# Linear attention followed by a SiLU layer pair: the order of all work in chunks 1 to 8 taken from a table

## Chip, cores and metric

One core of one Trainium2 chip. The metric is device microseconds (us) of one execution, from the first instruction to the last as the device counts it; lower is better. Profiles are of one execution each, and their span is about 2 us shorter than the time of the same execution. A run's state is "fast" or "slow" (lower granted TensorE clock for most of the execution); only fast runs are compared.

## The reference, cut to what matters

```python
# q, k, v: (8 batches, 8 heads, 576, 64);  w_in: (512, 2048);  w_out: (2048, 512)
q_s = softmax(q, axis=-1)                 # over the 64 features
k_s = softmax(k, axis=2)                  # over the 576 positions
kv  = einsum('bhsd,bhse->bhde', k_s, v)   # 64 x 64 per head
x   = einsum('bhsd,bhde->bhse', q_s, kv)  # to 4608 tokens x 512
h   = x @ w_in
out = (h * sigmoid(h)) @ w_out
```

## The kernel before

The 4608 tokens are cut into nine chunks: chunk 0 has 576 tokens, chunk 1 has 448, the rest 512. In chunk `t` TensorE does the first layer of chunk `t`, the second layer of chunk `t-1`, and, up to chunk 6, the attention of batch `t+1`. The attention of one batch runs through every engine: ScalarE takes exponentials of q and k, VectorE sums them, GpSimd normalises q and casts v, a DMA transposes q, TensorE makes kv (`kv`) and q·kv (`xt`), and ScalarE copies the latter to `XT`.

From chunk 2 on both layers use a seven-product scheme (Strassen's, in Winograd's form): VectorE forms sums of the inputs (`xsum`, `presum`), TensorE makes seven products, and the results are combined from PSUM by VectorE. First-layer blocks that don't use the scheme are called `mm1`. In these traces each engine takes its own instructions in program order, so the program order decides what an engine waits with. The program gives six PSUM banks to the ring from which `mm1`, `product1`, `kv` and `xt` draw, and two to the second layer.

```python
def product1(t, g, k):                  # one of seven first-layer products
    ...                                 # matmuls into a bank, then at once:
    if k == 1:                          # copy out of PSUM, ScalarE or VectorE
        if g in COPY_V: nc.vector.tensor_scalar_mul(out=new("s1"), in0=o, scalar1=1.0)
        else:           nc.scalar.activation(out=new("s1"), in_=o, func=ACT.Copy, scale=1.0)
    elif k == 6: add(new("u2"), MP[t, g, "s1"])      # VectorE: PSUM + SBUF
    elif k == 7: add(new("u3"), MP[t, g, "s1"])
    elif k == 2: silu(o, 0, 0)                       # ScalarE
    else:
        x = MP[t, g, {5: "u3", 4: "s1", 3: "u2"}[k]]
        add(x, x)                                    # VectorE, and its SiLU at once
        silu(x, *{5: (1, 1), 4: (1, 0), 3: (0, 1)}[k])
... # cut: the same pattern in product/after for layer two, stores through the SP queue

for b in range(4, B):   # what is done beside chunk b-1, by position in its list of units
    plan_attn(b, lambda i, f: plan(b - 1, i, f),
              (1, 1, 1, 1),   # four exponentials (q, q, k, k)
              (8, 10),        # q sums and q normalisations
              (6, 9),         # v casts
              11,             # DMA transpose of q
              (13, 16),       # kv products and their copies
              (20, 22),       # q.kv products and their copies
              11, 12)         # load of the next q; loads of the next k and v
```

The softmax here doesn't subtract the row's maximum and nothing guards it: scores larger than these inputs give would overflow.

## Time and profile before

| | before |
|---|---|
| time, median of 4 fast runs | 299.43 us (297.78 to 300.28) |
| span of the profile | 298.7 us |
| TensorE busy | 265.3 us, 89% |
| VectorE / ScalarE / GpSimd busy | 71% / 58% / 23% |

The first lines are of the page's first two parts: busy time by engine, and the granted TensorE clock in 40 equal slices (about 7.5 us each; 9 is 90% or more).

```profile
PE 265.3 (89%) x2546; PEld 187.6 (63%) x2546; DVE 211.0 (71%) x410; ACT 172.0 (58%) x275; POOL 69.7 (23%) x53
...
PEclk9999999997999689999999999999999999999999
```

TensorE idles 33 us, and the clock dips twice in mid-kernel, in slice 10 (67 to 75 us) and in slices 14 and 15 (97 to 112 us), each time at a pause of TensorE. The list of who TensorE waited for (total us, number of times, longest):

```profile
PE o L189 <- DMA qT<-eq: 9.3, 5, 5.5
PE hps L287 <- ACT s L315: 2.9, 4, 0.7
PE kvps L155 <- POOL vaug L100: 2.8, 1, 2.8
...
PE ops L379 <- ACT s L401: 2.1, 4, 0.5
...
PE hps L287 <- DVE s L313: 1.9, 4, 0.5
PE hps L287 <- DVE u L301: 1.4, 5, 0.6
```

`o` is q·kv, `qT` the transposed q, `hps` and `ops` the banks of layers one and two, `kvps` that of kv, `vaug` the cast v; `s` and `u` are PSUM copies and sums.

*Chunk 2.* The timeline of the DMA issues on the SP queue, around the longest wait (start, duration, what):

```profile
92.48 0.58 SPq L84 DMA_DIRECT2D qt<-in_q_dram  x1
93.17 5.93 SPq L124 DMA_TRANSPOSE qT<-eq  x1
```

and of TensorE, where q·kv starts at last:

```profile
102.56 0.48 PE L189 MATMUL o<-qT,kvn 64*64 64x320 bf16 x4 [5.51 <-DMA qT<-eq]
```

*Chunk 1.* GpSimd's timeline. `TW` are differences of weights; the gate holds GpSimd until VectorE has made its own weight differences `TX`.

```profile
54.17 0.17 POOL L614 CAST gate<-TX 1x1 f32<-1x1 bf16 x1 [16.10 <-DVE TX L262]
54.31 4.20 POOL L355 TENSOR_TENSOR TW<-W 128x1024 bf16<-128x1024 bf16 x2
58.48 4.21 POOL L355 TENSOR_TENSOR TW<-W,TW 128x1024 bf16<-128x1024 bf16 x2
62.65 4.18 POOL L113 TENSOR_TENSOR eq<-eq,rzq 128x1152 bf16<-128x1152 bf16 x2
66.79 2.24 POOL L100 CAST vaug<-vt 128x1152 bf16<-128x1152 f32 x2
```

kv needs the first cast; TensorE stands from 65.2 to 68.0.

*All chunks.* Length of each chunk, from its first first-layer matmul to the next chunk's (the last runs to the end of the span). It is read from the timeline of TensorE, and it is the measure used throughout:

| chunk | 0 | 1 | 2 | 3 | 4 | 5 | 6 | 7 | 8 and end |
|---|---|---|---|---|---|---|---|---|---|
| before, us | 32.6 | 27.1 | 30.6 | 31.4 | 30.2 | 31.2 | 30.2 | 25.8 | 43.3 |

Chunk 7 has the same products without kv and exponentials; chunks 3 to 6 are about 5 us longer, and some 1 us of that is kv.

### The profile page before, as it was taken

How to read it: one execution, taken by the hardware profiler on the slowest of the kernel's cores; microseconds unless marked ns; L12 is line 12 of the kernel's file. 1: busy time of each engine (PE TensorE's matmuls, PEld its weight loads, DVE VectorE, ACT ScalarE, POOL GpSimd, SP SyncE). 2: the span in 40 equal slices, each digit the busy share in tenths (PEclk: the TensorE clock that was granted, in tenths of full speed). 3: DMA queues.
4: the chain of work that ended last, by engine and by line, in shares of the span. 5: the costliest groups of instructions: out<-in, count | busy, mean ns of one | idle time of the engine just before them, and what ended most of it. 6: DMA issues, size and time to landing. Idle time of an engine off the chain costs nothing.

```text
span 298.7 us, 6269 instructions
## 1 busy us (share of the span) xinstructions
PE 265.3 (89%) x2546; PEld 187.6 (63%) x2546; DVE 211.0 (71%) x410; ACT 172.0 (58%) x275; POOL 69.7 (23%) x53
## 2 busy tenths in 40 slices
PE   8699989978989298879889988899899999999993
PEld 3366654434437156767677767676677787688782
DVE  3885767953256396968798879778788868867841
ACT  4774655842894388546955695459546456535300
POOL 0640400799362000700060016002420000000000
PEclk9999999997999689999999999999999999999999
DMA  7999999939409964089506970792052211301234
GB/s 241 297 200 279 307 256 322 343 126 234 163 0 220 221 254 160 1 151 379 170 2 121 333 232 13 119 341 81 0 102 63 59 38 35 72 1 37 70 72 105
DMA packets 42381, 46.48 MB, mean 156 GB/s; under 512 B 18544, under 2 KB 29808, under 8 KB 42352
## 3 DMA queue, kind: packets, MB, share of 16 engines
q1 hardware_dynamic: 37312, 38.35, 45.7%
q0 software_dynamic: 5040, 7.73, 11.7%
q8 instruction: 20, 0.33, 0.4%
q14 instruction: 9, 0.07, 0.1%
HBM read 36.70 MB, written 9.44 MB: 154 GB/s over the span
## 4 chain that ended last, share of the span: by engine, by line
PE 33%; DMA 19%; ACT 15%; DVE 13%; POOL 8%; issue 6%; SPq 3%; POOLq 1%; DVEq 0%; ACTq 0%
PE ops L379 15%; PE hps L287 8%; DMA W<-in_moe_w_out_dram 7%; DMA qT<-eq 7%; PE hps L209 5%; POOL eq L113 4%; PE ops L438 4%; DVE zq L107 4%; ACT ek L93 4%; ACT eq L93 3%; DVE u L301 3%; DMA kt<-in_k_dram 2%; ACT GT L234 2%; ACT L234 2%; DVE u L396 2%
## 5 line engine op out<-in xcount | busy, mean ns | idle before, releaser
L209 PE MATMUL hps<-XT,W 128*128 128x512 bf16 (+3 forms) x320 | 63.4, 338 | 1.8 <-ACT GT L234 1.3
L309 ACT ACTIVATE GT<-u 128x512 bf16<-128x512 f32 x40 | 25.1, 630 | 49.7 <-DVE u L301 49.7
L379 PEld LDWEIGHTS <-GT 128*128 128x128 bf16 x448 | 43.8, 98 | 10.4 <-issue 2.8
L209 PEld LDWEIGHTS <-W 128*128 128x128 bf16 x320 | 30.9, 98 | 26.4 <-issue 3.9
L113 POOL TENSOR_TENSOR eq<-eq,rzq 128x1152 bf16<-128x1152 bf16 x14 | 29.6, 2115 | 53.6 <-DVE rzq L108 35.2
L301 DVE SCALAR_TENSOR_TENSOR u<-hps,s 128x512 f32<-128x512 f32 x40 | 27.2, 683 | 18.5 <-PE hps L287 8.2
L379 PEld LDWEIGHTS <-SW 128*128 128x128 bf16 x336 | 32.8, 98 | 4.0 <-DVE SW L339 0.2
L287 PE MATMUL hps<-XS,TX 128*128 128x256 bf16 x240 | 34.6, 273 | 0.8 <-DVE u L301 0.8
L287 PEld LDWEIGHTS <-TX 128*128 128x128 bf16 x320 | 30.7, 99 | 7.0 <-issue 3.0
L230 DVE SCALAR_TENSOR_TENSOR GT<-sg,hps 128x320 bf16<-128x320 f32 (+3 forms) x64 | 23.7, 413 | 15.8 <-ACT sg L218 15.8
L438 PE MATMUL ops<-W,GT 128*128 128x512 bf16 x128 | 33.7, 387 | 1.1 <-DMA W<-in_moe_w_out_dram 0.9
L218 ACT ACTIVATE sg<-hps 128x320 f32<-128x320 f32 (+2 forms) x48 | 21.3, 454 | 20.2 <-PE hps L209 14.9
L379 PE MATMUL ops<-W,GT 128*128 128x256 bf16 x224 | 28.7, 272 | 2.1 <-ACT s L401 2.1
L287 PEld LDWEIGHTS <-W 128*128 128x128 bf16 x240 | 23.1, 99 | 11.6 <-issue 8.0
L100 POOL CAST vaug<-vt 128x1152 bf16<-128x1152 f32 x12 | 14.6, 1224 | 65.7 <-DMA vt<-in_v_dram 50.3
L379 PE MATMUL ops<-TW,SW 128*128 128x256 bf16 x224 | 28.8, 273 | 0.0
L301 DVE SCALAR_TENSOR_TENSOR u<-hps,u 128x512 f32<-128x512 f32 x40 | 27.0, 678 | 2.6 <-PE hps L287 1.8
L379 PE MATMUL ops<-TW,GT 128*128 128x256 bf16 x224 | 28.7, 273 | 0.0
L287 PE MATMUL hps<-XT,W 128*128 128x256 bf16 x160 | 23.9, 273 | 4.8 <-ACT s L315 2.9
L107 DVE TENSOR_REDUCE zq<-eq 128x18 f32<-128x1152 bf16 x16 | 21.5, 1344 | 8.4 <-ACT eq L93 8.4
L200 ACT CAST XT<-o 128x512 bf16<-128x512 f32 (+3 forms) x36 | 18.4, 560 | 11.0 <-PE o L189 11.0
L438 PEld LDWEIGHTS <-GT 128*128 128x128 bf16 x128 | 12.5, 99 | 14.1 <-issue 2.5
(68 smaller groups left out, 350.5 us busy)
## 6 DMA issues: line engine op xcount, KB each, us to landing
qt<-in_q_dram SPq DMA_DIRECT2D x6, 1152.0 KB, 5.9
kt<-in_k_dram SPq DMA_DIRECT2D x6, 1152.0 KB, 6.4
vt<-in_v_dram SPq DMA_DIRECT2D x6, 1152.0 KB, 8.7
W<-in_moe_w_in_dram POOLq DMA_DIRECT2D x4, 512.0 KB, 10.2
W<-in_moe_w_out_dram POOLq DMA_DIRECT2D x4, 512.0 KB, 17.8
out_dram<-oq SPq DMA_DIRECT2D x16, 128.0 KB, 3.6
out_dram<-u SPq DMA_DIRECT2D x30, 64.0 KB, 2.1
out_dram<-u SPq DMA_DIRECT2D x13, 128.0 KB, 2.4
```

What stands on the lines that cost most here:

```text
L93: nc.scalar.activation(out=o, in_=jgd(st[b][src], cc), func=ACT.Exp)
L107: nc.vector.reduce_sum(out=st[b]["zq"][:, cc], in_=e, axis=AX.X)
L113: eng.tensor_tensor(out=e, in0=e, in1=r[:, :, :, None].to_broadcast([128, J, 2, D]), op=ALU.mult)
L200: nc.scalar.copy(out=x, in_=o1[g][:, 0:size])
L209: nc.tensor.matmul(out=hps[:, 0:size], lhsT=W1[:, c, fb * 128:(fb + 1) * 128], rhs=XT[t][:, c, off:off + size], start=(c == 0), stop=(c == ...
L218: nc.scalar.activation(out=sg[:, 0:size], in_=hps[:, 0:size], func=ACT.Tanh, scale=0.5)
L230: nc.vector.scalar_tensor_tensor(out=y, in0=sg[:, h], scalar=1.0, in1=hps[:, h], op0=ALU.add, op1=ALU.mult)
L287: nc.tensor.matmul(out=o[:, f, :], lhsT=l(c, 2 * g + f), rhs=r(c), start=bool(first and f == 0 and c == 0), stop=(c == HK - 1), skip_group ...
L301: nc.vector.scalar_tensor_tensor(out=out, in0=o, scalar=1.0, in1=x, op0=ALU.mult, op1=ALU.add)
L309: nc.scalar.activation(out=y, in_=x, func=ACT.Silu)
L379: nc.tensor.matmul(out=o[:, a, :], lhsT=l(f), rhs=r(f), start=bool(first and a == 0 and f == 0), stop=(f == HF - 1), skip_group_check=True,)
L438: nc.tensor.matmul(out=OP[t, tb], lhsT=GT[t][:, fc, tb * 128:(tb + 1) * 128], rhs=W2[:, fc, :], start=(fc == 0), stop=(fc == NFB - 1),)
```

## The change

The intent: all of chunks 1 to 8 is placed by a table. Each chunk gives a position for every piece of work, and pieces that were glued together (a product, its sum, its SiLU, its store) get positions of their own. The core of the diff:

```diff
+STEADY = {'std': 1, 'order': [(1, 1), (1, 6), (1, 2), (1, 7), (1, 5), (2, 1), ...],
+  'ex': [-5.1, -2.59, -3.08, -3.57],          # exponentials q, q, k, k
+  'qs': [6.4, 6.9], 'qn': [6.91, 6.91], 'vs': [3.4, 9.92], 'tp': 7.9,
+  'lq': 10.95, 'lk': 13.9, 'lv': 11.41,       # loads of the next q, k, v
+  'sl': [0.5, 2.0, 6.5, 4.0],                 # SiLUs of the four plain blocks
+  'act': {(1, 5): 11.02, (1, 2): 6.55, ...},  # SiLUs held back
+  'xs': [-2.6, 0.4, 2.4, 1.9], 'pb': [-0.55, 0.46, 2.95, 1.46, 2.95], ...}
+for _t in range(3, 8):
+    PLAN[_t] = STEADY
+TXAT = [(0, 15.76), (0, 15.96), (1, -2.6), (1, -8.1)]          # VectorE's TX
+GATE = (1, 2.8)
+TWAT = [(1, 2.4), (1, 4.9), (1, 7.9), (1, 4.9), (1, 14.95), ...] # GpSimd's TW
... # tables of chunks 0, 1, 2, 8, 9 cut
-            if g in COPY_V:
+            if PLAN[t]["s1"][g]:        # one more copy per steady chunk on VectorE
... # product1 split into product1, sum1, silu1; mm1 into mm1, act1;
... # xt into xt, xtcopy; product into product, after
+    for l in todo:
+        for _, _, f, args in sorted(l, key=lambda x: x[:2]):
+            f(*args)
```

A position of -5.1 sorts to the front of the chunk's own list.

## The prediction

> **What bounds it now.** TensorE: busy 265.3 of 298.7 us (page, part 1). Its idle time (list of waits, timeline of its matmuls) falls into places that an order can reach:
>
> - Chunk 2: 5.5 us for the transposed q (DMA), whose issue at 93.17 took 5.93 us because a whole q load entered the same queue 0.7 us earlier. The granted clock falls to 0.68 in 100 to 110 us: an estimated 3 us more. The Trainium skill, "TensorE: Matmul & The Clock Gate", Part 1, says one idle window of about 3.4 us halves the clock; the trace agrees.
> - Chunk 1: 2.8 us for GpSimd's cast of v, behind four weight sums (2.1 us each) and two q normalisations that began only at 54.2 us, since a gate waits for a VectorE difference; a slow clock follows (0.88 in 70 to 80 us, about 1.5 us). At 87.8, 1.3 us for a SiLU: ScalarE was in 7 us of table loads and exponentials.
> - Chunks 3 to 6 last 31.4, 30.2, 31.2, 30.2 us (starts of their first matmuls); chunk 7, without attention, 25.8. Attention is about 1.3 us of matmuls, so about 27 is the floor. Each repeats the same waits: 0.5 + 0.2 + 0.5 + 0.3 + 0.7 behind the exponentials at its second position, and 0.4 to 1.6 for the transposed q; start to start, 3.4 to 4.5 us.
> - Chunks 7, 8: only 1 us. Start (17 us) and end (20 us) are not touched.
>
> **What the change does.** It adds no work, and places production, evacuation, SiLU and stores separately. Exponentials stand before the chunk (-5 to -2.6); q sum, normalisation and transpose move from positions 8 to 11 to 6.4 to 7.9, about 3 us earlier; from chunk 2 on the transpose precedes the q load; S sums move away from the v cast (a 0.41 us sum took 1.37 us beside it); SiLUs wait behind copies and sums that free banks. One more PSUM copy (0.68 us) per steady chunk goes to VectorE. GpSimd's weight sums are spread. Chunk 0 is nearly the old order rewritten.
>
> **What it costs.** VectorE is busy 24.9 us per steady chunk (busy time by stretch), ScalarE 20. At 27 us VectorE would be 92% busy, so I do not expect the floor; holding sums back also keeps some of the six banks. Estimate: 28 us.
>
> **Sum.** Chunks 3 to 6: 4 x 2.7 = 11. Chunk 2: 6 of about 9. Chunk 1: 3 of about 5.5. Chunks 7, 8: 0.5. Together about 20 us, nearly all on the critical path, since TensorE is the chain. Predicted 280 us, 8 in 10 between 273 and 289. Faster by over 2%: 0.92; within: 0.06; slower: 0.02.
>
> **What would show it.** TensorE's idle time about 15 instead of 33 us; no wait of q·kv on the transpose over 1 us; the transpose's issue in chunk 2 near 3 us; clock at least 0.95 everywhere after 20 us; steady chunks 28 us apart; VectorE near 90% in them; table loads still 12; time before 50 us unchanged.
>
> **What would make it wrong.** (a) VectorE or ScalarE, in strict order, is blocked by an early sum or exponential whose data is late (k load), and steady chunks stay near 30. (b) A bank held back stalls the ring. (c) In chunk 2 the k exponentials lie between SiLUs, so the 1.3 us wait returns. (d) In chunk 1 the q load still precedes the transpose. If all bite, 290; if the order fits perfectly, 270.

## More of the kernel before

Asked by stretch, the granted clock is 0.50 from 68.9 to 72.3 us and from 99.6 to 106.4 us.

*Chunk 4, one of the four steady ones (3 to 6).* ScalarE's timeline:

```profile
139.81 0.58 ACT L234 ACTIVATE GT<-hps 128x512 bf16<-128x512 f32 x1
140.40 1.28 ACT L93 ACT_TABLE_LOAD   x1
141.70 2.22 ACT L93 ACTIVATE eq<-qt 128x1152 bf16<-128x1152 f32 x2
143.82 2.20 ACT L93 ACTIVATE ek<-kt 128x1152 bf16<-128x1152 f32 x2
146.04 1.28 ACT L234 ACT_TABLE_LOAD   x1
147.33 1.57 ACT L234 ACTIVATE GT<-hps 128x512 bf16<-128x512 f32 x3
148.78 0.62 ACT L401 ACTIVATE s<-ops 128x512 f32<-128x512 f32 x1
```

The chunk's first matmul started at 138.18. The exponentials stand behind its first SiLU; the copy `s`, which frees a bank of layer two, comes 10.6 us after that matmul. Later in the same chunk comes one of the four waits of the list's second line, for a first-layer copy `s`:

```profile
152.33 0.63 ACT L309 ACTIVATE GT<-u 128x512 bf16<-128x512 f32 x1 [2.44 <-DVE u L301]
...
154.09 0.60 PE L287 MATMUL hps<-XT,W 128*128 128x256 bf16 x4 [0.73 <-ACT s L315]
```

The copy itself starts at 153.46, behind two SiLUs. These had waited 2.44 us for sums of VectorE, which stood behind a q sum (1.34 us, at 150.04) and, before it, behind a wait of VectorE for the layer-two copy (1.51 us). The 2.44 us and the 0.73 us are the same in all four steady chunks; chunks 7 and 8, without a q sum, don't have the wait.

## The result, and the profile after

| | before | after |
|---|---|---|
| time, median of 4 fast runs | 299.43 us | 276.84 us (276.09 to 278.42) |
| ratio | | 0.926 (95% interval 0.920 to 0.932) |
| span of the profile | 298.7 | 274.1 |
| TensorE busy / idle | 265.3 / 33.4 | 261.6 / 12.5 |

Ratios here are the mean time of one kernel's fast runs over that of the other's fast runs of the same rounds, so not quite the ratio of the medians quoted.

```profile
PE 261.6 (95%) x2546; PEld 186.8 (68%) x2546; DVE 218.1 (80%) x417; ACT 167.8 (61%) x268; POOL 70.4 (26%) x53
...
PEclk9979999999999999999999999999999999999998
```

TensorE's idle time falls by 20.9 us, and its busy time by 3.7 although it does the same work. The two dips of the clock in mid-kernel are gone; TensorE was busy for 7.2 us of them, at half the clock, an estimated loss of 3.6 us. The dip in the third slice, 3.4 us long, lies in chunk 0 and costs an estimated 1.7 us; a second profile of the same kernel, below, does not have it. The rest of the 3.7 us is not explained here. TensorE's longest waits now:

```profile
PE hps L317 <- ACT GT L264: 2.5, 3, 1.6
PE kvps L169 <- ACT vaug L112: 1.8, 2, 1.1
```

No wait over 0.2 us on the transposed q, on the cast v of chunk 1, or on a copy `s` is left; the first line is new. In chunk 2 the transpose goes before the q load, and its issue is half as long:

```profile
84.96 2.86 SPq L138 DMA_TRANSPOSE qT<-eq  x1
87.87 0.57 SPq L98 DMA_DIRECT2D qt<-in_q_dram  x1
```

In chunk 1 GpSimd starts three microseconds earlier, and two weight differences instead of four precede the normalisations:

```profile
50.98 0.84 POOL L644 CAST gate<-TX 1x1 f32<-1x1 bf16 x1 [9.64 <-DVE TX L292]
51.78 2.11 POOL L386 TENSOR_TENSOR TW<-W 128x1024 bf16<-128x1024 bf16 x1
53.97 2.13 POOL L386 TENSOR_TENSOR TW<-W,TW 128x1024 bf16<-128x1024 bf16 x1
57.49 4.20 POOL L127 TENSOR_TENSOR eq<-eq,rzq 128x1152 bf16<-128x1152 bf16 x2 [1.38 <-ACT sg L248]
61.64 2.13 POOL L386 TENSOR_TENSOR TW<-W,TW 128x1024 bf16<-128x1024 bf16 x1
63.71 2.25 POOL L114 CAST vaug<-vt 128x1152 bf16<-128x1152 f32 x2
```

ScalarE in chunk 4, whose first matmul starts at 122.29:

```profile
123.06 1.28 ACT L107 ACT_TABLE_LOAD   x1
124.35 1.16 ACT L107 ACTIVATE eq<-qt 128x1152 bf16<-128x1152 f32 x1
126.72 2.22 ACT L107 ACTIVATE ek<-kt 128x1152 bf16<-128x1152 f32 x2 [1.20 <-DMA kt<-in_k_dram]
128.84 1.15 ACT L107 ACTIVATE eq<-qt 128x1152 bf16<-128x1152 f32 x1
130.00 1.28 ACT L264 ACT_TABLE_LOAD   x1
131.30 1.09 ACT L264 ACTIVATE GT<-hps 128x512 bf16<-128x512 f32 x2
132.27 0.60 ACT L434 ACTIVATE s<-ops 128x512 f32<-128x512 f32 x1
```

Now `s` stands behind two SiLUs instead of four, and starts 10.0 us after the chunk's first matmul instead of 10.6. The exponentials start 2.1 us after it instead of 3.5. But ScalarE waits 1.2 us for the k load in mid-block (2.2 us in chunk 5), and the SiLUs behind it are what TensorE's new wait is for.

| chunk | 0 | 1 | 2 | 3 | 4 | 5 | 6 | 7 | 8 and end |
|---|---|---|---|---|---|---|---|---|---|
| before, us | 32.6 | 27.1 | 30.6 | 31.4 | 30.2 | 31.2 | 30.2 | 25.8 | 43.3 |
| after, us | 33.0 | 23.4 | 21.3 | 28.1 | 27.9 | 28.9 | 27.1 | 25.7 | 42.2 |
| gain | -0.4 | 3.7 | 9.3 | 3.4 | 2.3 | 2.3 | 3.0 | 0.0 | 1.0 |

So 11.0 of the 24.6 us of span lie in the four steady chunks, 9.3 in chunk 2 and 3.7 in chunk 1. The two profiled executions took 300.64 and 276.09 us, the one slower and the other faster than its kernel's median, so the profiles differ by 2 us more than the medians (22.6 us). The experiments ask which part of the table earned them.

### The profile page after: what moved, and what is told of

It reads as the page before. It is cut to its first block, busy times and chain, and to the rows that moved or that the text cites. A ratio compares the mean times of both kernels' runs of the same rounds, so it can differ in the third digit from the quotient of the medians.

```text
span 274.1 us, 6282 instructions
## 1 busy us (share of the span) xinstructions
PE 261.6 (95%) x2546; PEld 186.8 (68%) x2546; DVE 218.1 (80%) x417; ACT 167.8 (61%) x268; POOL 70.4 (26%) x53
## 4 chain that ended last, share of the span: by engine, by line
PE 61%; DMA 12%; ACT 8%; DVE 8%; SPq 4%; issue 3%; POOL 2%; ACTq 0%; POOLq 0%; DVEq 0%
PE ops L410 21%; PE hps L234 16%; PE hps L317 14%; DMA kt<-in_k_dram 9%; PE ops L474 8%; DMA vt<-in_v_dram 3%; ACT ek L107 2%; SPq L98 2%; PE kvps L169 2%; SPq L463 2%; DVE u L334 2%; ACT L264 1%; ACT eq L107 1%; POOL eq L127 1%; PE o L204 1%
## 5 line engine op out<-in xcount | busy, mean ns | idle before, releaser
L410 PEld LDWEIGHTS <-GT 128*128 128x128 bf16 x448 | 43.4, 98 | 8.6 <-issue 1.0
L234 PEld LDWEIGHTS <-W 128*128 128x128 bf16 x320 | 31.6, 100 | 25.5 <-issue 1.6
L334 DVE SCALAR_TENSOR_TENSOR u<-hps,s 128x512 f32<-128x512 f32 x40 | 27.1, 681 | 8.7 <-PE hps L317 6.4
L474 PE MATMUL ops<-W,GT 128*128 128x512 bf16 x128 | 31.8, 379 | 0.0
L248 ACT ACTIVATE sg<-hps 128x320 f32<-128x320 f32 (+2 forms) x48 | 21.3, 456 | 15.5 <-PE hps L234 10.4
L410 PE MATMUL ops<-TW,SW 128*128 128x256 bf16 x224 | 28.0, 273 | 0.0
L121 DVE TENSOR_REDUCE zq<-eq 128x18 f32<-128x1152 bf16 x16 | 21.3, 1329 | 4.9 <-ACT eq L107 4.9
L107 ACT ACTIVATE ek<-kt 128x1152 bf16<-128x1152 f32 x16 | 18.1, 1158 | 5.6 <-DMA kt<-in_k_dram 5.6
```

Of the source, the lines that this page charges most:

```text
L107: nc.scalar.activation(out=o, in_=jgd(st[b][src], cc), func=ACT.Exp)
L121: nc.vector.reduce_sum(out=st[b]["zq"][:, cc], in_=e, axis=AX.X)
L234: nc.tensor.matmul(out=hps[:, 0:size], lhsT=W1[:, c, fb * 128:(fb + 1) * 128], rhs=XT[t][:, c, off:off + size], start=(c == 0), stop=(c == ...
L248: nc.scalar.activation(out=sg[:, 0:size], in_=hps[:, 0:size], func=ACT.Tanh, scale=0.5)
L334: nc.vector.scalar_tensor_tensor(out=out, in0=o, scalar=1.0, in1=x, op0=ALU.mult, op1=ALU.add)
L410: nc.tensor.matmul(out=o[:, a, :], lhsT=l(f), rhs=r(f), start=bool(first and a == 0 and f == 0), stop=(f == HF - 1), skip_group_check=True,)
```

## The experiments

The theory held after the result, as in the prediction (A): the steady chunks gain because the exponentials no longer stand in second place, where their 7 us hold up copies and sums. Rivals: (B) the earlier transpose of q; (C) SiLUs held behind copies and sums. For chunks 2 and 1: the place of the q load, and GpSimd's order. They ran in three sets, each set on one chip and beside the kernel before: e3, e4, e5, e8 (301.0 us for the kernel before), e1, e2, e6, e7 (301.1) and e9 to e12 (300.4). The headings give these labels. Only the third set holds the new kernel itself (e9); in the first two, "slower" and "faster" are against its 276.84 us from another chip. By the ratios to the kernel before, which differ by 1.6 us between its own two sets of runs, e3 comes out 4.6 us faster than the new kernel, e4 2.4, e1 2.0 and e7 9.7 us slower. Single microseconds are therefore read from chunk lengths where that is possible. For the edits of the old order, the old order was first written as a table; its instructions then stand in the same order as those of the kernel before on every engine.

### e3: exponentials put back to second place

```diff
+STEADY['ex'] = [0.9, 0.901, 0.902, 0.903]
```

> The new order, with only the four exponentials of chunks 3 to 6 put back to second place in the chunk. Theory A (what the steady chunks gained, about 2.7 us each, comes mainly from having the exponentials in front): the waits of TensorE on s and u sums and copies come back, 1.5 to 2.2 us a chunk, 6 to 9 us in all, so 283 to 286 us. Theory B (it comes from the earlier transpose of q) and theory C (from holding SiLUs back): under 2 us slower, 277 to 279; and if the late k load is what limits the new order, it may even be equal, since the exponentials then no longer wait 1.2 to 2.2 us for k.

Measured: 274.09 us, ratio to before 0.911 (0.906 to 0.915), where the new kernel has 0.926. Chunks 3 to 6 took 28.1, 27.0, 27.8, 27.0 us. Putting the exponentials back makes the kernel 2.8 us *faster* than the new order's 276.84, on a chip where the kernel before was 1.5 us slower. Theory A falls: the place of the exponentials is not what was gained. ScalarE's wait for k fell from 5.6 to 2.0 us over the whole run, as the rival had allowed; the front place had only moved the exponentials ahead of their data. In time the two places are close: in chunk 4 the first exponential starts 3.0 us after the first matmul here and 2.1 us in the new kernel. What the front place is worth once k comes in time is not tested by itself; chunks 4 to 6 then take 26.8 us each (e12 below) against 27.0, 27.8 and 27.0 here, where ScalarE still waits some for k.

### e8: only the exponentials moved, in the old order

```diff
+for t in range(3, 7):
+    PLAN[t]['ex'] = [-5.1, -3.57, -3.08, -2.59]    # all else in the old order
```

> The old order (instruction for instruction that of the kernel before on every engine) with only the exponentials of chunks 3 to 6 moved in front of the chunk, in the order q, q, k, k. Theory A: the 2.2 us of waits behind the exponential block go, the waits on the transpose stay: 4 to 8 us faster than the kernel before, 291 to 295 us. Theories B and C: within 2 us of the kernel before.

Measured: 299.94 us, ratio 0.999 (0.992 to 1.006). No gain. TensorE's waits on `s` and `u` are about those of before (8.3 us in all, as before). ScalarE's timeline in its chunk 4 (first matmul at 140.67) says why:

```profile
141.76 0.63 ACT L407 ACTIVATE GT<-u 128x512 bf16<-128x512 f32 x1 [1.82 <-DVE u L385]
...
143.70 2.22 ACT L158 ACTIVATE eq<-qt 128x1152 bf16<-128x1152 f32 x2
...
149.34 2.06 ACT L315 ACTIVATE GT<-hps 128x512 bf16<-128x512 f32 x4
151.26 0.63 ACT L485 ACTIVATE s<-ops 128x512 f32<-128x512 f32 x1
```

ScalarE, in strict order, reaches the block only behind the last SiLU of the chunk before, which itself waits 1.8 us for VectorE. "In front of the chunk" thus moves the first exponential from 3.5 to 3.0 us after the chunk's first matmul, and one more SiLU then stands between the block and `s`: `s` still starts 10.6 us after that matmul. The run shows that this edit gains nothing; what exponentials that really start earlier would be worth it cannot show.

### e4: the transpose of q put back

```diff
+STEADY.update(qs=[7.9, 9.9], qn=[7.91, 9.91], tp=10.9)
```

> The new order, with only the q sums, q normalisations and the transpose of chunks 3 to 6 put back to their old places (7.9, 9.9, 10.9). Theory B (the earlier transpose is most of the gain): 6 us or more slower, 283 or more. Theory A: a wait of q.kv on the transpose of 0.5 to 1.5 us a chunk returns, so 1 to 4 us slower in all, 278 to 281, with no new waits on s and u sums.

Measured: 281.07 us, ratio 0.934 (0.929 to 0.938): 4.2 us slower than 276.84, just above what A allowed and below what B asked for. Chunks 3 to 6 sum to 117.2 us against 111.9 in the new kernel's profile. Two waits came:

```profile
PE o L205 <- DMA qT<-eq: 3.2, 3, 1.3
PE hps L318 <- DVE u L335: 2.2, 5, 0.5
```

The first was expected. The second was not: a q sum, 1.34 us on VectorE, now stands in front of a `u` sum for which TensorE waits. So the earlier q chain is worth 4 to 5 us of the steady chunks' 11 (2.4 by the ratios), in two ways.

### e5: SiLUs not held back

```diff
+STEADY.update(act={}, add={}, ya={}, sl=[0, 1, 2, 3])
```

> The new order, with every SiLU of chunks 3 to 6 issued straight behind what produces its input, and the last store sum as well. Theory C (holding SiLUs back is most of the gain): 5 us or more slower, 282 or more. Theory A: SiLUs wait in strict order for sums but ScalarE is only 65 to 70 percent busy, so within 1.5 us, 275.5 to 278.5.

Measured: 278.16 us (276.75 to 279.43), ratio 0.923 (0.917 to 0.929); by medians 1.3 us slower than 276.84, by ratio equal. It is not the main part (C falls as a whole), but its mechanism is plain; one wait of the kernel before returned, once in each steady chunk:

```profile
PE ops L411 <- ACT s L435: 3.1, 4, 0.9
```

Four SiLUs again stand in front of the copy that frees the layer-two bank. The profiled execution was the slowest of the four, and its steady chunks sum to 115.2 us, 3.3 more than the new kernel's; the medians say 1.3. About half of the difference is the clock: from 163.4 to 166.8 us it was 0.50 while TensorE was busy throughout, an estimated loss of 1.7 us, and the three other executions ran at a higher mean clock (0.995 to 1.0 against 0.985). So holding SiLUs is worth 1 to 2 us, up to 3 when the clock dips, and these runs don't fix it closer. (The edit's `add={}` changes nothing: in the steady table its entries name products that have no sum. The sums themselves were hardly held back.)

### e10: VectorE's input sums put back

```diff
+STEADY.update(xs=[-0.08, 0.92, 1.92, 2.92], pb=[0.915, 0.916, 1.915, 1.916, 2.915])
```

> The new order, with VectorE's S sums and layer-two sums at the start of chunks 3 to 6 put back to the old places (after the first, second and third first-layer block, in one row). Theory D (a part of the steady gain is that the s copy and u sums, which free PSUM banks, no longer stand behind eight bf16 sums on VectorE): a wait of TensorE of 0.6 to 0.9 us on VectorE's s copy and u sum returns in each chunk, 2 to 4 us slower than the new kernel. If the old places cost nothing in the new surroundings: under 0.7 us.

Measured: 276.33 us, beside 276.25 for the unchanged new kernel on the same chip (below). It costs nothing that can be told apart: TensorE's waits on VectorE's `u` and `s` rise from 0.2 to 0.8 us in all.

### e1: the q load in front of the transpose, in chunk 2 alone

```diff
+PLAN[2]['lq'] = 5.85        # was 5.95; the transpose stands at 5.9
```

> The new order, with one change in chunk 2: the load of the next q is issued just before the transpose of q, as in the kernel before, instead of just behind it. Theory A (the 5.9 us issue of the transpose before came from the q load in the same queue): the issue goes from 2.9 to 5 to 6 us, q.kv of chunk 3 waits 1.5 to 4 us for it, 1.5 to 4 us slower in all. Rival (the issue was long for another reason, such as stores or other loads): issue stays near 3 us and the time within 1 us.

Measured: 280.99 us, ratio 0.933 (0.930 to 0.936); 4.1 us slower than 276.84. The SP queue:

```profile
84.84 0.58 SPq L99 DMA_DIRECT2D qt<-in_q_dram  x1
85.54 5.77 SPq L139 DMA_TRANSPOSE qT<-eq  x1
```

The issue doubles from 2.86 to 5.77 us with nothing changed but the load in front of it, q·kv waits 2.7 us, and the clock falls to 0.7 and 0.8 in two slices. Chunk 2 grows from 21.3 to 25.7 us. That the load's place in front makes the issue long is shown. By what way is not: in chunk 0 the transpose's issue takes 4.7 to 6.0 us in both kernels and in this run with no load issued on that queue in the 33 us before, while other transfers keep the DMA engines busy, so traffic alone may do it.

### e2: the transpose in front of the q load, in the old order

```diff
+PLAN[2]['tp'] = PLAN[2]['lq'] - 0.0005     # all else in the old order
```

> The old order, with one change in chunk 2: the transpose of q is issued just before the load of the next q. Theory A: issue near 2.9 us at about 92.5, landing near 97.5 instead of 102.5, so q.kv waits 0.5 to 1.5 us instead of 5.5, the pause is too short to lower the clock: 5 to 8 us faster than before, 291 to 294.5. Rival (the exponentials and the normalisation of chunk 2 came too late, and the store issues in front of the transpose held it): 0 to 3 us faster, the low clock stays.

Measured: 297.18 us, ratio 0.988 (0.984 to 0.992): 3.9 us faster than the 301.12 beside it, between the two expectations. The issue took 2.84 us, q·kv waited 1.95 us, the clock stayed up. Chunk 2 shrank by 4.9 us, and chunk 3 grew by 0.9 (TensorE then waits there 1.5 us for `s`). So this one swap makes about half of chunk 2's 9.3 us. The rest goes with the earlier q exponentials and normalisation, as far as the traces tell: in the new kernel GpSimd ends them at 80.9, in the old at 90.2, and the wait for a SiLU of 1.3 us at 87.8 is gone. No run undid these.

### e7: the old weight differences in chunk 1, a first try

```diff
+TXAT[:] = [(0, 15.76), (0, 15.96), (1, 0.9), (1, 1.9)]
+TWAT[:] = [(1, 2.801)] * 4 + [(1, 11.801)] * 4
```

> The new order, with only the weight differences of chunks 0 and 1 (VectorE's four, the gate, GpSimd's eight) put back to their old places. Theory A (the v cast of chunk 1 came late behind four weight sums on GpSimd that began late): the wait of kv on the cast returns, 2 to 4 us, with a slow clock behind it: 3 to 5 us slower. Rival (chunk 1 gained by its exponentials and by the matmuls of the second layer put at its end): under 1 us.

Measured: 288.65 us, ratio 0.958 (0.955 to 0.962), 11.8 us slower, three times what was expected. The edit was not what it was meant to be: in the new table the v casts stand at 11.8 and 11.9, so four differences fell *between* them, which neither kernel has.

```profile
PE kvps L217 <- POOL vaug L162: 10.8, 2, 8.1
```

8.1 us of this is that artifact; the other wait, 2.7 us on the first cast, is the one of the kernel before.

### e11: the old weight differences, mended

```diff
+TXAT[:] = [(0, 15.74), (0, 15.96), (1, 0.9), (1, 1.9)]
+TWAT[:] = [(1, 2.801)] * 4 + [(1, 11.95)] * 4
```

> The first try at the old weight sums put four of GpSimd's sums between the two v casts of chunk 1, which neither kernel has, and cost 8.2 us there. This one is the old order of GpSimd: gate, four sums, two normalisations, both casts, four sums. The wait of kv on the cast should be 2.9 us as in the kernel before, chunk 1 should grow from 23.4 to 26 to 27.5 us, 3 to 4 us slower than the new kernel in all. If the first-layer blocks that come before kv cover the wait: under 1 us.

Measured: 281.18 us, median of the three fast runs from 280.19 to 282.26 (the fourth was slow); ratio 0.937 (0.931 to 0.943); 4.9 us slower than the unchanged new kernel beside it. GpSimd's order in chunk 1, with VectorE's differences that it waits for, is worth all of that chunk's 3.7 us and more. The profile (clock 0.85, span 303.7) cannot show how the 4.9 us divide. The profiles of the kernel before, of e2 and of e8, which all have the old weight differences, show the same two things: a wait of 2.8 us on the first cast and, within 1 us of its end, 3.4 us at a clock of 0.50, an estimated 1.7 us more.

### e9: the new kernel again

> The new kernel, unchanged, to stand on the same chip as the three beside it. 276 to 278 us; chunk lengths as in its first profile except where ScalarE waits for k, which may vary by 1 us a chunk with the loads.

Measured: 276.25 us, ratio 0.921 (0.916 to 0.925). Chunks 3 to 6: 28.1, 28.4, 27.7, 27.6 us, where the first profile had 28.1, 27.9, 28.9, 27.1: the sum is the same (111.7 and 111.9), the longest one moves with the wait for k.

### e6 and e12: the k load in front of the v load

Two runs, the first with the exponentials' order changed too.

```diff
+STEADY.update(lk=11.41, lv=13.9, ex=[-5.1, -3.57, -3.08, -2.59])   # first run
+PLAN[2].update(lk=6.4, lv=12.91)                                   # (as it was)
+STEADY.update(lk=11.41, lv=13.9)                                   # second run
```

> A try at a faster kernel: the new order, with the k load issued before the v load, in chunks 2 to 6, and the exponentials of chunks 3 to 6 in the order q, q, k, k. ScalarE waits 1.2 to 2.2 us for k in the new order and TensorE 0.5, 0.7 and 1.8 us behind that. If that wait is the cause, those go: 1.5 to 3 us faster than the new order, 274 to 275.5 us. If VectorE (90 percent busy) is what sets the chunk, within 0.7 us of it. It may also be that v, then late, holds the cast and kv back.

> The new order, with only the k load issued before the v load in chunks 3 to 5 (in chunk 2 it already is); the order of the exponentials, q, k, k, q, stays. If the order of the two loads is what made ScalarE wait for k: ScalarE's wait for k goes and steady chunks are 26.8 to 27.2 us, 3 to 4 us faster than the new kernel. If the order of the exponentials is needed too (k is asked for one exponential too early): 1 to 2 us faster, with waits for k of about 1 us left.

Measured: 272.51 us with both, ratio 0.905 (0.902 to 0.908); 272.74 us with the loads alone, ratio 0.909 (0.905 to 0.912), beside 276.25 for the new kernel on the same chip: 3.5 us faster. In both, chunks 4 to 6 take 26.8 us each. The order of the two loads is the whole of it; ScalarE in chunk 4 of the second run:

```profile
124.50 1.16 ACT L110 ACTIVATE eq<-qt 128x1152 bf16<-128x1152 f32 x1
125.57 2.20 ACT L110 ACTIVATE ek<-kt 128x1152 bf16<-128x1152 f32 x2
127.68 1.15 ACT L110 ACTIVATE eq<-qt 128x1152 bf16<-128x1152 f32 x1
```

No gap is left. These two are the fastest kernels. VectorE, at over 90% of a 26.8 us chunk, was not what held the new order at 28. In a stretch of one chunk's length TensorE is now busy throughout (columns as explained in the next section):

```profile
121.90:148.70 26.80, 26.80 (x303) 21.42 (x301) 24.39 (x47) 19.40 (x30) 7.08 (x4) 1.00 0.63 189
```

## Why the prediction was right, and where its reasons were not

280 us was predicted, 273 to 289 as the range; 276.84 was measured. Term by term, with what the chunk lengths show:

| term | predicted gain | measured |
|---|---|---|
| chunks 3 to 6 | 4 x 2.7 = 11 us | 11.0 |
| chunk 2 | 6 | 9.3 |
| chunk 1 | 3 | 3.7 |
| chunks 0, 7, 8 and end | 0.5 | 0.6 |

- **Bound by TensorE's waits: right.** Idle time was to be about 15 us and is 12.5. The signs named for it all came: no wait on the transpose, its issue 2.86 us in chunk 2, steady chunks 28.0 us apart in the mean, twelve table loads, the first 49 us unchanged, no dip of the clock after 20 us except in the last slice. VectorE's busy time in chunk 4, from the busy times by stretch, is 25.5 of 27.8 us, 92%:

```profile
122.30:150.10 27.80, 27.16 (x302) 21.39 (x300) 25.47 (x46) 19.45 (x30) 6.66 (x4) 1.00 0.65 184
```

  (The columns are stretch and length, then busy us of TensorE, its weight loads, VectorE, ScalarE and GpSimd, then clock, DMA share and GB/s.)
- **Steady chunks: the size right, a reason wrong.** The prediction put five of the waits "behind the exponentials at its second position". That step failed. Moved to the front in the old order, the exponentials gained nothing, and moved back in the new order they gained 2.8 us. In place of it the runs showed the earlier q chain (4.2 us, part of it because a q sum no longer stands in front of a `u` sum) and, with 1 to 3 us, the copy placed before two of the SiLUs. That 28 us a chunk came out as estimated is luck in part: the estimate gave VectorE's load as the limit, and what held the chunks there was the late k. Nothing that was undone brought back the wait of before on the first-layer copy `s` (2.9 us in all). Its chain in the kernel before, shown above, needs two things at once: SiLUs in front of the copy, and their sums behind a q sum. e5 put back the first alone (the SiLU there waits 1.3 us, TensorE not at all) and e4 the second alone (the copy then stands in front of the waiting SiLU). So the two changes together may have removed it, as may the new order of the products or the places of the second layer's products; no run puts both back, and that part of the 11 us stays open.
- **Chunk 2: the term mis-sized.** 6 us of "about 9" were claimed, and 9.3 came. The mechanism, a q load in front of the transpose, is shown in both directions (4.1 and 3.9 us of time, 4.4 and 4.9 us of chunk 2). The prediction held 3 us back, among other things for a SiLU wait that might return (its item c); none did. Its estimate of 3 us for the slow clock looks too large: the swap in the old order shortened the wait by 3.6 us and chunk 2 by 4.9, which leaves some 1.3 for the clock within that chunk. The trace of the kernel before agrees: of the 6.8 us at a clock of 0.50, TensorE was busy for only 3.8, an estimated loss of 1.9 us, since the dip had begun during the pause.
- **Chunk 1: right in kind.** 3 us were claimed, 3.7 came, and undoing the order of the weight differences alone costs 4.9.
- **The doubts.** The prediction named "exponentials in front of the chunk may wait for the k load", in its item (a). That happened, and cost 3.5 us by the last run. It held VectorE's load responsible for not reaching "about 27 is the floor"; that was wrong, for with the k load earlier the chunks reach 26.8 us.

Of the Trainium skill, "TensorE: Matmul & The Clock Gate", Part 1, says that an idle window of about 3.4 us halves the clock. It was used for the clock's dips. The runs agree on the half (0.50) and that a pause of 5.5 us brings it; but it also came with pauses of 2.7 and 2.8 us and, in e8, of 2.05 us, and not with one of 1.95 us, so the length of a single pause does not decide it here. "ScalarE: Activation LUTs", What ACT_TABLE_LOAD costs, gives 1283 ns for a table load; the traces show 1283 ns too.

## What to carry to other kernels

An instruction's place in the program is not its place in time: on an engine that runs in strict order, "earlier" starts no earlier than the wait in front of it ends, and data not yet there turns "earlier" into a stall for all that follows, so look first at what the instruction would wait for at its new place. On a queue shared by loads, stores and a transpose, put first what is needed first: two swaps of neighbouring DMA issues (transpose before q load, k load before v load) were worth about 4 and 3.5 us. When a table moves everything at once, a right total does not prove the reasons; undo the parts one by one, and compare the engine's order with both kernels before trusting such an undo.

## What the Trainium skill lacked or had wrong

- "DMA: Bandwidth & Descriptors", § DMA Transpose (X-bar), does not say what a plain load in front of a transpose does to it: with a 1152 KB load issued 0.7 us earlier on the same queue, the issue took 5.77 and 5.93 us, and 2.84 and 2.86 us with the load behind it. In chunk 0, with no load on that queue for 33 us but other transfers under way, it took 4.69 to 6.00 us.
- "TensorE: Matmul & The Clock Gate", Why this matters for your kernels, warns of idle gaps over about 3 us. Here a gap of 2.7 us (with one of 0.4 us that ended 0.7 us before it) went with a clock of 0.50 for 6.8 us, gaps of 2.8 us and one of 2.05 us with 3.4 us of it, and one of 1.95 us with none; in e5 3.4 us of it came after two gaps of only 0.97 and 0.87 us.
- "ScalarE: Activation LUTs", § What ACT_TABLE_LOAD costs, adds a drain of about 1380 ns, 2.66 us in all per switch. The load itself took 1.28 us here, and the exponential started 1.29 us after the load did (123.06 to 124.35); no drain is to be seen in the timeline.
- "TensorE: Matmul & The Clock Gate", Part 1, says that one or two busy cores never trip the peak-current limiter. That limiter takes the clock to 13/16 (0.81). One execution of this one-core program ran at a granted clock of 0.85 nearly throughout (305.62 us against 281.18); whether that is the same limiter, and what the chip's other cores did then, is not known.
